# A spectral filter fused with a gated feed-forward: the forward sine table exchanged by DMA instead of TensorE

## The chip, the cores and the metric

The kernel runs on one core of a Trainium2 chip. TensorE (PE) does matrix products, VectorE (DVE) and ScalarE (ACT) do element-wise work and move results out of PSUM, GpSimd (POOL) does small integer and constant work, SyncE (SP) issues every DMA. The metric is the device time of one execution in microseconds (us). "Faster" or "slower" always means against the kernel before.

## The reference

```python
def _A_ref(x, w_r, w_i):
    X = rfft2(x.astype(float32), axes=(-2, -1))
    X = X * (w_r + 1j * w_i)
    return irfft2(X, s=(S, D), axes=(-2, -1)).astype(bfloat16)

def _B_ref(x, w_gate, w_up, w_down):
    return (_gelu(x @ w_gate) * (x @ w_up)) @ w_down

x = A_x                          # 1 x 2048 x 640, bfloat16
xn = _layernorm(x, axis=-1)
s = _A_ref(xn, A_w_r, A_w_i)
g = _silu(_B_ref(xn, B_w_gate, B_w_up, B_w_down))    # F = 1536
return x + s * g
```

A row-wise layer norm feeds two branches. One is a two-dimensional Fourier transform over 2048 rows and 640 columns, a product with a complex filter, and the transform back. The other is a feed-forward network with a GELU gate. Their product is added to the input.

## The kernel before

The 2048 rows are held as 16 slabs X[:, n1, :] of 128 rows. A 2048-point transform along the rows is split into 128 points times 16 points.

**Feed-forward.** Four groups of four slabs. For each group, `ffn_piece` (L707) makes 12 tiles of gate and up products (L714), ACT applies GELU (L718), VectorE multiplies (L720). `down_third` (L729) multiplies with the down weights (L738). xnT, the transposed normalized input of a group, comes from `slab_T` (L458): the first four slabs by TensorE, the other twelve by a DMA transpose that SyncE issues (L465).

**Forward spectral part.** VectorE folds pairs of slabs (L443 to L453). `slab_S1` (L480) does the 128-point step along the rows: five matmuls per slab into pz (L484) whose moving operand is the slab's block Tfwd[:, n1, :] of a sine table. `group_D` (L504) does the step along the columns (pd, L494 and L498) and stores Z to a DRAM scratch ZDR (L512).

**16-point phase.** `load_B2` (L524) reads ZDR back in another layout (L530); it starts when the last Z store has landed. Then eleven bursts: `s2_in` (px, L556) transforms, ACT evicts (L564), VectorE multiplies with the filter W1 and W2 (L568), `s2_out` (pu, L583) transforms back, and the result goes to a second scratch. Burst 0 begins at place `sb` of the plan below. `load_V` and the whole inverse part are placed relative to `sb`.

**Inverse part.** `slab_S1i` (L626) uses the blocks Tinv[:, n1, :] of the inverse table (pv, L631). `group_Di`, `group_cs` and `group_Y` follow, and `finish` (L682) multiplies and adds (L689, L690) and stores to the output (L691).

**The tables.** Integer phases in vt are made by GpSimd and VectorE. `tinv_sin` (L319) turns all 16 blocks into Tinv, 128 x 2048, in one ACT instruction (L320). `tfwd(h)` (L322) makes the forward table: it transposes eight 128 x 128 blocks of Tinv on TensorE (L326) into a PSUM tile, and VectorE copies them into Tfwd (L327). It is called for h = 0 and 1.

**Filter loads.** `w_rows(i, hh, ri, pm)` (L112) loads an eighth of filter W1 (i = 0) or W2 (i = 1): two DMAs, or three where one is cut in two (L118, L120, L121, L123), about 160 KB each. k = 0 to 7 stands for the eight calls that load W1, k = 8 to 15 for W2. GpSimd halves the edge columns of W1 and W2 (L127, `w_edge`).

**The order of the work** is written out by hand. `back` is a list of 144 pieces of feed-forward work (places 0 to 143). After place s of that list the program issues what `put(s, ...)` filed there, in the order of the `put` calls. A place is one third of a down product (8 matmuls) or one gate or up tile (5 matmuls). Places 24 to 35 are the down products of group 0, 36 to 59 the gate and up tiles of group 1, and 60 to 71 its down products. Every engine's instructions, and SyncE's DMA issues, keep the order of the places.

The places that matter here, before the change: `w_rows` of k = 0 to 7 at places 8 to 15, one each; `slab_T` of slabs 4 to 7 at 17, 19, 21 and 23; `tinv_sin` at 23; `tfwd` at 26 and 27; `slab_S1` of slab 0 at 30, of 1 to 3 at 32 to 34, of 4 to 6 at 37 to 39, of 7 to 9 at 42 to 44, of 10 to 12 at 47 to 49; `slab_T` of slab 8 at 32; `load_B2` at 56; `sb` = 65.

Of the kernel before, what the change touches and what calls it, by code (L numbers as in the profile page):

```python
# [10 lines left out]
BF16 = mybir.dt.bfloat16  # L11
INT32 = mybir.dt.int32
ACT = mybir.ActivationFunctionType
ALU = mybir.AluOpType
P = 128
# [11 lines left out]
TWO_PI = 2.0 * math.pi  # L27
# [4 lines left out]
def kernel(  # L32
# [40 lines left out]
    with tc.manual_schedule():  # L73
        build(nc, locals())


def build(nc, env):
    consts, big, wts, xg, work, psA, psB = (env[k] for k in ("consts", "big", "wts", "xg", "work", "psA", "psB"))
# [51 lines left out]
    Tinv = consts.tile([P, NS, P], BF16)  # L130
    Tfwd = consts.tile([P, NS, P], BF16)
# [5 lines left out]
    ident = consts.tile([P, P], BF16)  # L137
# [4 lines left out]
    def gtile(shape, dt):  # L142
        n = 1
        for k in shape:
            n *= k
        w = n if dt != BF16 else n // 2
        ap = GEN[:, goff[0]:goff[0] + w]
        goff[0] += w
        assert goff[0] <= NH * L // 2
        if dt != INT32:  # L150
            ap = ap.bitcast(dt)
        if len(shape) > 1:
            names = "abcdefg"[:len(shape)]
            ap = ap.rearrange("p (%s) -> p %s" % (" ".join(names), " ".join(names)), **dict(zip(names, shape)))
        return ap

    def c1(name, dt=FP32):
        return consts.tile([P, 1], dt, name=name)
# [44 lines left out]
    negpi = c1("negpi")  # L203
# [13 lines left out]
    vt = gtile([NS, P], INT32)  # L217
# [98 lines left out]
    def silu_table():  # L316
        nc.scalar.activation(out=warm, in_=negpi, func=ACT.Silu)

    def tinv_sin():  # L319
        nc.scalar.activation(out=Tinv, in_=vt, func=ACT.Sin, bias=negpi, scale=TWO_PI / 2048.0)  # L320

    def tfwd(h):  # L322
        sl = slice(8 * h, 8 * h + 8)
        pt = psB.tile([P, 8, P], BF16, tag="b")
        for k in range(8):
            nc.tensor.transpose(out=pt[:, k, :], in_=Tinv[:, 8 * h + k, :], identity=ident)  # L326
        nc.vector.tensor_copy(out=Tfwd[:, sl, :], in_=pt)  # L327

    fv = gtile([10, LH], FP32)
    ftm = gtile([5, LH], FP32)  # L330
# [464 lines left out]
    def put(s, *item):  # L795
        plan[s].append(item)
# [24 lines left out]
    put(17, stats, 8)  # L821
    put(19, stats, 9)
    put(23, fold_a, 0)
    for it in ((silu_table,), (tinv_sin,), (ft_sin, 0)):
        put(23, *it)
    put(24, fold_b, 0)
    put(28, mg_mask)
    put(25, root, 8, 2)
    put(25, fold_a, 1)
    put(26, tfwd, 0)  # L830
    put(27, tfwd, 1)
    put(27, norm, 8)
    put(28, fold_b, 1)
    put(29, stats, 10)
# [24 lines left out]
    for pair in range(6):  # L859
        b = F0 + 3 * pair + (0 if pair < 4 else 3)  # L860
        put(b, fold_a, pair + 2)
        put(b + 1, fold_b, pair + 2)
    z_end = F0 + 26
# [1 line left out]
        put(32 + 3 * k, slab_T, 8 + k, 2)  # L865
        put(65 + 3 * k, slab_T, 12 + k, 2)
    for k in range(16):
        put(8 + k if k < 8 else (32, 35, 38, 41, 44, 44, 47, 47)[k - 8], w_rows, k // 8, k % 8 // 4, k % 2, k % 4 // 2)
    put(40, w_edge, 0)
    put(z_end + 4, w_edge, 1)  # L870
    put(z_end, load_B2)
    put(z_end + 3, mg_turn)
    sb = z_end + 9
    for b in range(len(BURSTS)):
        put(sb + 24 * b // 11, s2_in, b)
        if b > 0:
# [69 lines left out]
```

## Time and profile before

| | before |
|---|---|
| median of 3 runs | 204.14 us (204.1 to 204.27) |
| the profiled execution's own time | 204.42 us |
| its span (first to last instruction) | 202.6 us |
| PE / DVE / ACT / POOL busy | 195.6 / 129.3 / 122.4 / 33.4 us |
| granted TensorE clock | 1.000 |
| DMA | 31.77 MB, mean 157 GB/s, hardware queue 71.4% of 16 engines |

The span is what the profile sees; the execution's own time has some 1.8 us around it. "Busy" is the sum of an engine's working time. Matrix products are pipelined, so a row's mean duration (219 ns for 128 columns) is longer than the pitch at which such products follow one another. The chain of work that ended last is traced back from the last instruction, at each step to what released it. A wait in SyncE's own list is one in front of a DMA issue. "To landing" is the time from the start of a DMA's issue until its data has arrived. A releaser can be named wrongly where a wait has several semaphores.

### The profile page before, as it was taken

What the parts mean: (1) busy time and instruction counts of PE and PEld (TensorE: products, weight loads), DVE (VectorE), ACT (ScalarE), POOL (GpSimd) and SP (SyncE); (2) the same over time, 40 slices, a digit from 0 to 9 for tenths busy, and PEclk for the clock granted to TensorE, in tenths of its full rate; (3) what the DMA queues carried; (4) which work ended last, traced back from release to release, by engine and by line L of the source; (5) the groups of instructions that cost most, each with busy time, mean ns of one, the idle gap of its engine ahead of it and who ended that gap; (6) DMA issues with size and microseconds to landing.
All of it is one profiled execution on the core that took longest, in us unless ns stands there. A gap on an engine that the chain in (4) does not pass through costs nothing.

```text
span 202.6 us, 4209 instructions
## 1 busy us (share of the span) xinstructions
PE 195.6 (97%) x1574; PEld 119.8 (59%) x1589; DVE 129.3 (64%) x340; ACT 122.4 (60%) x208; POOL 33.4 (16%) x61
## 2 busy tenths in 40 slices
PE   7899999999999999999999999999999999999993
PEld 5688854777555555566644333457775555556762
DVE  7886966786488982533576465342358776867672
ACT  2448657857886768423788688425375647476631
POOL 5327779953000200100000000000000000000000
PEclk9999999999999999999999999999999999999999
DMA  5999999899799999729995233569501334224211
GB/s 167 306 297 305 372 310 142 158 147 137 153 170 143 173 174 174 180 43 226 213 228 111 44 97 101 130 164 317 172 0 68 97 102 127 69 92 144 86 69 60
DMA packets 43315, 31.77 MB, mean 157 GB/s; under 512 B 12192, under 2 KB 41504, under 8 KB 43296
## 3 DMA queue, kind: packets, MB, share of 16 engines
q1 hardware_dynamic: 43296, 31.52, 71.4%
q8 instruction: 12, 0.20, 0.4%
q14 instruction: 7, 0.06, 0.1%
HBM read 21.66 MB, written 7.88 MB: 146 GB/s over the span
## 4 chain that ended last, share of the span: by engine, by line
PE 90%; DVE 4%; DMA 2%; issue 1%; POOL 1%; SPq 0%; ACT 0%; DVEq 0%
PE psu L714 25%; PE psg L714 24%; PE psg L738 13%; PE psu L738 12%; PE pd L494 5%; PE pz L484 2%; PE pv L631 2%; PE pu L583 2%; DMA X<-in_A_x_dram 2%; PE px L556 2%; PE pd L498 2%; DVE st L174 1%; DVE uT L720 1%; POOL rst L190 1%; PE pt L326 0%
## 5 line engine op out<-in xcount | busy, mean ns | idle before, releaser
L714 PE MATMUL psu<-xnT,Wu 128*128 128x512 bf16 (+2 forms) x289 | 60.9, 339 | 0.6 <-issue 0.2
L714 PE MATMUL psg<-xnT,Wg 128*128 128x512 bf16 (+2 forms) x286 | 60.4, 338 | 0.9 <-issue 0.5
L720 DVE TENSOR_TENSOR uT<-psu,ge 128x512 bf16<-128x512 f32 (+2 forms) x59 | 34.3, 585 | 29.8 <-PE psu L714 22.5
L718 ACT ACTIVATE ge<-psg 128x512 bf16<-128x512 f32 (+2 forms) x59 | 30.5, 518 | 27.6 <-PE psg L714 25.9
L738 PEld LDWEIGHTS <-uT 128*128 128x128 bf16 x384 | 36.3, 98 | 14.6 <-issue 0.6
L714 PEld LDWEIGHTS <-Wu 128*128 128x128 bf16 x295 | 26.6, 98 | 22.9 <-issue 2.7
L714 PEld LDWEIGHTS <-Wg 128*128 128x128 bf16 x295 | 26.6, 98 | 21.9 <-issue 1.5
L738 PE MATMUL psg<-Wd,uT 128*128 128x320 bf16 (+1 forms) x192 | 30.3, 302 | 0.0
L738 PE MATMUL psu<-Wd,uT 128*128 128x320 bf16 (+1 forms) x192 | 29.2, 296 | 0.0
L568 DVE TENSOR_TENSOR X<-xs,W 128x972 bf16<-128x972 bf16 (+2 forms) x22 | 13.3, 646 | 10.6 <-ACT xs L564 10.6
L174 DVE BATCH_NORM_STATS2 st<-X 128x6 f32<-128x320 bf16 x32 | 14.2, 482 | 0.5 <-DMA X<-in_A_x_dram 0.3
L633 ACT CAST W<-pv 128x640 bf16<-128x640 f32 x16 | 11.1, 692 | 5.4 <-PE pv L631 5.4
L510 ACT CAST GEN<-pd 128x966 bf16<-128x966 f32 (+1 forms) x10 | 10.4, 1102 | 5.3 <-PE pd L498 5.3
L656 ACT ACTIVATE W<-pd 128x960 bf16<-128x960 f32 (+2 forms) x14 | 10.1, 780 | 5.0 <-PE pd L498 5.0
L486 ACT CAST GEN<-pz 128x640 bf16<-128x640 f32 x16 | 11.0, 697 | 3.2 <-PE pz L484 3.2
L589 ACT CAST X<-pu 128x486 bf16<-128x486 f32 (+4 forms) x22 | 12.3, 558 | 0.3
L564 ACT CAST xs<-px 128x972 bf16<-128x972 f32 (+2 forms) x11 | 10.3, 936 | 2.4 <-PE px L556 2.4
L190 POOL TENSOR_TENSOR rst<-ve,mhalf 128x1 f32<-128x1 f32 (+2 forms) x9 | 6.5, 717 | 29.5 <-DVE ve L188 29.5
L662 DVE TENSOR_TENSOR W<-W 128x960 bf16<-128x960 bf16 (+1 forms) x12 | 6.8, 599 | 4.8 <-ACT W L656 4.8
L689 DVE TENSOR_TENSOR Yall<-Yall,G 128x640 bf16<-128x640 bf16 (+3 forms) x18 | 8.1, 450 | 2.1 <-ACT G L743 1.9
L747 DVE SCALAR_TENSOR_TENSOR G<-th,psu 128x320 bf16<-128x320 f32 x8 | 3.9, 488 | 8.4 <-ACT th L746 8.4
L452 DVE TENSOR_TENSOR f<-uvt 128x512 bf16<-128x512 bf16 x16 | 6.7, 421 | 3.0 <-PE pz L484 2.9
(137 smaller groups left out, 202.5 us busy)
## 6 DMA issues: line engine op xcount, KB each, us to landing
ZDR<-GEN SPq DMA_DIRECT2D x16, 160.5 KB, 5.3
xt<-in_A_x_dram SPq DMA_DIRECT2D x8, 320.0 KB, 3.5
UDR<-X SPq DMA_DIRECT2D x10, 240.8 KB, 3.6
W<-in_A_w_r_dram SPq DMA_DIRECT2D x14, 160.5 KB, 7.7
W<-in_A_w_i_dram SPq DMA_DIRECT2D x14, 160.5 KB, 6.0
out_dram<-Yall SPq DMA_DIRECT2D x14, 160.0 KB, 1.8
B<-ZDR SPq DMA_DIRECT2D x8, 240.8 KB, 5.5
Vin<-UDR SPq DMA_DIRECT2D x6, 321.0 KB, 6.3
```

The lines of the kernel that those rows point to most:

```text
L174: nc.vector.bn_stats(out=st[:, k, :], in_=X[:, n1, 320 * k:320 * k + 320])
L486: nc.scalar.copy(out=Zt[n1], in_=pz)
L494: nc.tensor.matmul(out[a][g], lhsT=lhs[a][:, g, :], rhs=T[:, g, 0:w], start=(a == 0), stop=False)
L510: ev(out=zd.rearrange("p a c (m b) -> p a c m b", b=2)[:, :, :, :, b], in_=pd[b])
L564: nc.scalar.copy(out=xs, in_=px[:, :, 0:n * w].rearrange("p k (h l) -> p k h l", l=w))
L568: nc.vector.tensor_tensor(out=pp[-1], in0=xs, in1=WT[:, :, h0:h0 + n, l0:l0 + w], op=ALU.mult)
L589: nc.scalar.copy(out=us[:, :, :, c0:c0 + (w + 1 - m) // 2], in_=pv[:, :, :, m:w:2])
L633: nc.scalar.copy(out=vs, in_=pv)
L714: nc.tensor.matmul(ps, lhsT=WT[:, c, t * P:(t + 1) * P], rhs=xnT[g][:, c, c0:c1_], start=(c == 0), stop=(c == 4))
L718: nc.scalar.activation(out=ges[t], in_=ps, func=ACT.Gelu_apprx_tanh)
L720: nc.vector.tensor_tensor(out=uT[g][:, t, c0:c1_], in0=ps, in1=ges[t], op=ALU.mult)
L738: nc.tensor.matmul(ph, lhsT=uT[g][:, t, j * P:(j + 1) * P], rhs=Wd[:, t, c0:c1_], start=(t == 0), stop=(t == NT - 1))
```

## The change

The forward table's blocks are turned by four DMA transposes (SyncE's queue) of four blocks each, straight from Tinv into Tfwd, with no PSUM tile and no copy. The sine is computed in two halves of eight blocks. The transfers stand at places 23 to 26, behind the sine. The filter loads k = 4 to 7 move from places 12 to 15 to places 27 to 30. The 16-point phase, and with it the loads and pieces of the inverse part, stands one place later (`sb` = 66).

```diff
-    def tinv_sin():
-        nc.scalar.activation(out=Tinv, in_=vt, func=ACT.Sin, bias=negpi, scale=TWO_PI / 2048.0)
-
-    def tfwd(h):
+    def tinv_sin(h):
         sl = slice(8 * h, 8 * h + 8)
-        pt = psB.tile([P, 8, P], BF16, tag="b")
-        for k in range(8):
-            nc.tensor.transpose(out=pt[:, k, :], in_=Tinv[:, 8 * h + k, :], identity=ident)
-        nc.vector.tensor_copy(out=Tfwd[:, sl, :], in_=pt)
+        nc.scalar.activation(out=Tinv[:, sl, :], in_=vt[:, sl, :], func=ACT.Sin, bias=negpi, scale=TWO_PI / 2048.0)
+
+    def tfwd(q):
+        sl = slice(4 * q, 4 * q + 4)
+        nc.sync.dma_start_transpose(out=Tfwd[:, sl, :], in_=Tinv[:, sl, :].rearrange("p n k -> p (n k)"))
...
-    for it in ((silu_table,), (tinv_sin,), (ft_sin, 0)):
+    for it in ((silu_table,), (tinv_sin, 0), (tinv_sin, 1), (ft_sin, 0)):
         put(23, *it)
...
-    put(26, tfwd, 0)
-    put(27, tfwd, 1)
+    for q in range(4):
+        put(23 + q, tfwd, q)
...
     for k in range(16):
-        put(8 + k if k < 8 else (32, 35, 38, 41, 44, 44, 47, 47)[k - 8], w_rows, k // 8, k % 8 // 4, k % 2, k % 4 // 2)
+        put((8 + k if k < 4 else 23 + k) if k < 8 else (32, 35, 38, 41, 44, 44, 47, 47)[k - 8], w_rows, k // 8, k % 8 // 4, k % 2, k % 4 // 2)
...
-    sb = z_end + 9
+    sb = z_end + 10
```

## The prediction

> **What bounds the kernel now.** I read the page first: shares by engine, then the chain of work that ended last.
>
> ```profile
> PE 195.6 (97%) x1574; PEld 119.8 (59%) x1589; DVE 129.3 (64%) x340; ACT 122.4 (60%) x208; POOL 33.4 (16%) x61
> ...
> PE 90%; DVE 4%; DMA 2%; issue 1%; POOL 1%; SPq 0%; ACT 0%; DVEq 0%
> ```
>
> TensorE is busy for 97% of the span and is 90% of the chain. A TensorE instruction removed after about 14 us shortens the span by its pitch; a wait put in front of one lengthens it by its length, for nothing later has slack to give back. So two questions decide: what the removed transposes took on TensorE, and whether the first matmul that reads Tfwd has to wait. Second view: the chain in order of time (start, length), around the exchange.
>
> ```profile
> 38.48 0.45 PE pt L326 x8
> 38.93 1.09 PE psg L738 x8
> 40.02 0.45 PE pt L326 x8
> ...
> 42.63 1.09 PE psg L738 x8
> 43.72 0.28 PE pz L484 x5
> ```
>
> Both groups of eight transposes stand on the chain, 0.45 us each, and the first reader of Tfwd (pz, L484, place 30) follows closely. TensorE's timeline has that matmul's start at 43.56, as does the list of Tfwd's users. Third view: SyncE's queue, since the new transfers are issued there.
>
> ```profile
> 34.38 0.57 SPq L123 DMA_DIRECT2D W<-in_A_w_r_dram  x1
> 35.52 3.41 SPq L118 DMA_DIRECT2D W<-in_A_w_r_dram  x4
> 38.98 2.74 SPq L123 DMA_DIRECT2D W<-in_A_w_r_dram  x4
> 41.89 7.95 SPq L465 DMA_TRANSPOSE xnT<-X  x4
> 49.94 0.53 SPq L512 DMA_DIRECT2D ZDR<-GEN  x1
> 50.56 1.21 SPq L465 DMA_TRANSPOSE xnT<-X  x1
> ```
>
> SyncE runs late. The eight issues from 35.52 to 41.7 are filter loads k = 4 to 7, asked for at places 12 to 15; the four transposed slabs behind them (slab_T of 4 to 7, places 17 to 23) go out at 41.89 to 49.83, though their data was normalized by 33.4 (ACT's timeline, L434). An issue starts when the eighth before it has landed: the load at 28.77 starts as Wd lands (18.34 + 10.4), the one at 35.52 as the load of 23.17 lands (+ 12.3).
>
> **The change, part by part.**
>
> *Transposes off TensorE.* 16 matmuls, 2 x 0.45 = **-0.90 us** on the chain. With everything before it unchanged, pz would be reached at 43.56 - 0.90 = 42.66.
>
> *Copies off VectorE, sine in two.*
>
> ```profile
> L320 ACT ACTIVATE Tinv<-GEN,negpi 128x2048 bf16<-128x2048 int32 x1 | 2.0, 1987 | 0.0
> ...
> L327 DVE COPY Tfwd<-pt 128x1024 bf16<-128x1024 bf16 x2 | 1.4, 692 | 1.0 <-PE pt L326 1.0
> ```
>
> VectorE loses 2 x 0.69 us; it waits on TensorE here, so 0. The sine of 128 columns (L397) takes 0.392, of 2048 1.987: 0.83 ns a column and 0.29 fixed. Each part is then 1.14, ACT carries +0.29, and the first part ends at 36.20 + 1.14 = 37.34. ACT's next evictions (L743, 38.85 and 39.17) go 0.3 later; their banks are written again at 42.5 or later, so 0. Without that cover it would cost 0.3.
>
> *SyncE's order.* With k = 4 to 7 at places 27 to 30, SyncE reaches slab_T(4) at 35.52. Then come slab_T 5, 6, 7, the four Tfwd transfers (places 23 to 26), the eight issues of k = 4 to 7, the Z store of place 31 and slab_T(8). Only the first transfer is urgent: it holds slabs 0 to 3. The others are read at places 37, 43 and 49, 8 us and more later.
>
> When does it land? Its source (37.34) is not the limit; four slab transfers ahead of it are. *Early end:* each issues in 1.22 us when nothing holds it (1.23 at 48.60, 1.21 at 50.56), 1.27 with the step between: 35.52 + 4 x 1.27 = 40.6. The new transfer has four blocks instead of five, an estimated 0.97 from 1.22. The slab issued at 48.60 landed 2.76 later, 1.53 after its issue ended. So 40.6 + 0.97 + 1.53 = 43.1. *Late end:* the four slabs did not issue freely; they took 7.95 us and stood behind seven unfinished filter loads. Then the last filter load landed at 41.11 + 7.8 = 48.9 and the fourth slab's issue ended at 49.83, 0.92 after it. Now too seven loads are unfinished at 35.52, the last landing at 34.38 + 6.3 = 40.7. That gives 41.6, and 41.65 + 0.97 + 1.53 = 44.15. If the transfer took the median of line 465 (5.2) or its longest (8.8) it would land at 46.9 or 50.5; those stood in a fuller queue. I take 44.0, near the second value, because the queue ahead is the same in kind and number. The stall at pz is 44.0 - 42.66 = **+1.3 us**; bounds 0.4 and 1.5, far ends 4.2 and 7.8. Behind pz in TensorE's order is everything else, so all of it counts.
>
> Here a rule of the Trainium skill speaks against the change. "VectorE: DVE Perf Modes", section "The three transpose paths", gives 1309 ns for one 128x128 block by DMA against 390 ns on TensorE, and advises TensorE. By it four blocks are an estimated 5.2 us, the landing would be 46.9 and the sum +3.1 instead of +0.2. The trace disagrees on both: 0.45 us for eight blocks on TensorE, and the last two slabs of five blocks land 0.65 us apart (45.88 + 4.84 and 48.60 + 2.76).
>
> *Filter loads later.* The four loads occupied the queue for some 8.2 us (landings 40.7 to 48.9) and now do so from about 47 to 55.4. W1 is first read after 94, so its own lateness costs 0. POOL's edge scaling (L127, 50.28) waits to about 56 with the root for slabs 12 and 13 behind it, due at place 41, about 58: covered. But stores and loads behind them go 2 to 3 us later. What absorbs this (busy per engine, then clock, DMA share, GB/s):
>
> ```profile
> 51.40:58.00 6.60, 6.55 (x55) 3.49 (x54) 3.11 (x11) 5.90 (x8) 0.00 (x0) 1.00 0.88 177
> 58.00:82.00 24.00, 23.71 (x204) 13.85 (x204) 17.84 (x46) 16.60 (x23) 1.59 (x2) 1.00 1.14 166
> 82.00:85.00 3.00, 2.84 (x26) 1.43 (x26) 1.49 (x3) 1.78 (x2) 0.52 (x1) 1.00 0.48 107
> ```
>
> The queue is full from 58 to 82 and half empty from 82 to 85, before the last Z stores (83.8, waiting for VectorE): some 1.5 us of room there and 0.8 before 58. I take 0; bounds 0 and +1.
>
> *16-point phase a place on.* A place here is eight down matmuls, 1.09 us. Its first matmul waits for B now: five matmuls of burst 0 span 0.83 where those of burst 1 span 0.40.
>
> ```profile
> 93.52 0.83 PE L556 MATMUL px<-B,MG 64*64 64x162 bf16 x5
> ...
> 96.55 0.40 PE L556 MATMUL px<-B,MG 64*64 64x159 bf16 x5
> ```
>
> The spacing beyond an ordinary tile change is 0.2 us; the place removes it: **-0.2**, and leaves B about 0.9 us for being late. All later pieces move by one place as well, TensorE's amount unchanged. At the end VectorE's last group (193.43 to 197.11) goes 1.09 later, to 198.2, still ahead of the last product at 198.79: 0, and 0.1 if it slips that far.
>
> *Sum:* -0.90 + 1.3 + 0 - 0.2 = **+0.2 us**. The profiled execution took 204.42 (span 202.6, 1.8 around it), so 204.6 for it; it ran 0.28 over the median of the runs, 204.14, which becomes **204.35**.
>
> **Rivals.**
>
> *In time (faster).* The slabs issue freely once k = 4 to 7 are gone, and the transfer lands by 43.3. For it: 1.21 to 1.23 us per issue in two rows. Against: the slabs issued at 43.42 and 45.88 took 2.36 and 2.63, with a like queue ahead. Stall 0.4 to 0.65, sum about -0.6: 203.5.
>
> *Late transfer (slower).* The first transfer lands like the median of its kind, 5.2 us after issue, at 46.9; TensorE stands at pz for 4.2 us. Sum 4.2 - 0.9 - 0.2 = +3.1: 207.2. It decides from a landing later than 44.15: beyond that the stall eats the gain and 0.4 more. For it: median 5.2. Against: by then the queue ahead is only slabs. The page above says the same time.
>
> *Backlog reaches B (slower).* The 2 to 3 us by which the queue lags at 56 do not find room; the last Z stores, then B, land 2 us late. TensorE comes to px at 93.52 + 1.09 + 0.4 (the changed sum ahead) = 95.0, B's second part at 93.95 + 2: stall 1.0, sum +1.2: 205.35. Against: the half-empty stretch at 82 to 85.
>
> *Doesn't do it:* the transfers would wait behind filter loads after all. SyncE issues in the order of the places, so I give it nothing.
>
> **How the numbers follow.** About 0.2% (0.41 us) is what a measurement of this kernel can tell from no change. Forecast 0.42, of which 0.36 within 0.2% and 0.06 slower; in time 0.28; late transfer 0.15; backlog 0.15. Faster 0.28, same 0.36, slower 0.36. The forecast's own range is 203.75 to 204.75, from stalls of 0.7 to 1.7. To hold 8 in 10 the range takes in the first rival and the third and part of the second: 203.4 to 206.5.
>
> **What would show it.** No line 326 or 327; slab_T(4) issued at 35.5; the first new transfer issued at 40.6 to 41.7 and landed at 43.1 to 44.2; a gap before the first pz of 0.4 to 1.5 us, none before the later ones; px of burst 0 as short as burst 1's; the last Z stores within 1 us of where they were. The forecast is wrong if the gap at pz is under 0.7 or over 1.7, or if px of burst 0 waits.

## The result, and the profile after

The changed kernel takes 212.62 us (median of six executions, 209.87 to 214.51) against 204.12 for the kernel before beside it: ratio 1.0364, 95% interval 1.0328 to 1.0399. Ratios, here and in the table below, leave out executions over 1.5% slower than the fastest of the same kernel, two of the six here, which is why 3.64% (7.4 us) is less than the 8.5 us between the medians. The forecast was no clear change, 204.35 us; the changed kernel is slower and lies outside the stated range. In all six executions the mean granted clock is below full, 0.976 to 0.992. The profiled execution took 213.03 us, its span is 211.1. Line numbers behind `tfwd` are two lower in the changed kernel: pz is L482, px L554, the slab transposes L463, the new transfers L325.

The page of the changed kernel (busy time by engine, the granted clock in 40 slices, the chain by engine):

```profile
PE 198.9 (94%) x1573; PEld 119.7 (57%) x1573; DVE 127.7 (60%) x338; ACT 122.2 (58%) x209; POOL 33.7 (16%) x61
...
PEclk9999999999999999999599999999999999999999
...
PE 67%; DMA 18%; DVE 7%; SPq 3%; issue 1%; ACT 1%; POOL 1%; DVEq 0%
```

TensorE was 90% of the chain and is now 67%. DMA has 18%, and in one slice the clock is at a half. The chain in order of time and SyncE's list show the exchange itself:

```profile
42.32 1.09 PE psg L736 x8
43.40 0.28 PE pz L482 x5
```

```profile
35.04 5.36 SPq L463 DMA_TRANSPOSE xnT<-X  x4
40.50 5.16 SPq L325 DMA_TRANSPOSE Tfwd<-Tinv  x4
45.70 3.57 SPq L118 DMA_DIRECT2D W<-in_A_w_r_dram  x4
49.32 2.56 SPq L123 DMA_DIRECT2D W<-in_A_w_r_dram  x4
51.99 0.54 SPq L510 DMA_DIRECT2D ZDR<-GEN  x1
```

The transposes are gone from the chain and pz follows the down product without a pause. The first transfer, issued at 40.50, landed 2.5 us later, at 43.0, just ahead of its reader at 43.24. Where the time went stands 50 us later, at the first matmuls of the 16-point phase (TensorE's timeline; in brackets the idle time before and its releaser):

```profile
94.41 1.25 PE L736 MATMUL psg<-Wd,uT 128*128 128x320 bf16 x8
99.40 0.55 PE L554 MATMUL px<-B,MG 64*64 64x162 bf16 x3 [3.74 <-DMA B<-ZDR]
100.58 0.61 PE L554 MATMUL px<-B,MG 64*64 64x486 bf16 x2 [0.64 <-DMA B<-ZDR]
```

TensorE waits 4.4 us for B. The columns of the next view are PE, PEld, DVE, ACT and POOL busy, then the granted clock, the DMA share (the times of packets overlap, so it can exceed 1) and GB/s:

```profile
97.00:99.00 2.00, 0.00 (x0) 0.00 (x0) 0.00 (x0) 0.00 (x0) 0.00 (x0) 1.00 0.93 228
99.00:106.40 7.40, 6.37 (x35) 3.22 (x36) 1.95 (x4) 2.07 (x4) 0.00 (x0) 0.54 1.09 209
106.40:109.00 2.60, 2.60 (x29) 1.61 (x25) 1.46 (x4) 2.20 (x4) 0.00 (x0) 1.00 1.06 219
```

After the wait the clock is at 0.54 for 7.4 us (at 0.50 for 6.8 of them). That takes 7.4 x 0.46 = 3.4 us at most; TensorE stood idle for 0.64 us of it, so some 3.1 us of work is lost. The Trainium skill, "TensorE: Matmul & The Clock Gate", Part 1, states that an idle window of some 3.4 us halves the clock until a busy one has passed. The trace agrees: 3.74 us of idle did it, and the waits of 0.6 to 1.3 us in the profiles below did not.

The account against the profile of before: 4.4 of wait for B less the 0.4 there was, 3.1 of clock, 0.56 at another stall, -0.90 for the transposes, +0.57 at the start of the execution (the second group of transposes of the input begins at 9.02 instead of 8.45, in code that is unchanged; in the runs below it begins at 8.07 to 8.34, so this belongs to the one execution). That is 7.3 of the 8.5 us between the spans; some 1.2 is spread over smaller waits.

Why is B late? The same view of the changed kernel, and then of the kernel before:

```profile
41.00:48.00 7.00, 7.00 (x66) 5.15 (x65) 4.92 (x17) 4.61 (x10) 3.96 (x11) 1.00 0.54 84
48.00:58.00 10.00, 10.00 (x88) 6.06 (x85) 6.25 (x21) 8.38 (x12) 0.86 (x1) 1.00 1.16 161
58.00:82.00 24.00, 23.41 (x201) 13.47 (x200) 17.11 (x46) 16.10 (x23) 2.12 (x3) 1.00 1.23 161
82.00:92.00 10.00, 9.74 (x74) 5.68 (x73) 4.03 (x8) 3.06 (x5) 0.52 (x1) 1.00 1.21 173
```

```profile
41.00:48.00 7.00, 7.00 (x64) 5.08 (x62) 4.77 (x17) 4.89 (x10) 3.00 (x10) 1.00 1.37 122
...
82.00:92.00 10.00, 9.84 (x75) 6.08 (x75) 4.03 (x8) 3.26 (x6) 0.52 (x1) 1.00 0.47 111
```

From 41 to 48 us the DMA engines are half idle (share 0.54) where they were full (1.37). SyncE spends that time issuing transposes, 1.3 us each with the step between, and up to 45.70 nothing else is issued. The DMA lines of the changed kernel from 41 to 48 us, in 40 slices of 0.175 us, show it:

```profile
DMA  9300799600029992000799600079999400000000
GB/s 215 55 0 1 161 222 212 145 8 0 0 51 224 212 211 52 0 0 1 157 221 219 142 9 0 0 154 197 205 196 43 0 0 3 7 10 9 10 9 0
```

Each of the four transfers moves data for some 0.7 of its 1.3 us. The moved loads are issued from 45.70 on, but from 46.4 to 48 almost nothing moves (0 to 10 GB/s), and the first of them lands at 50.4. By slab_T(8) the queue is 5.9 us late (landing 59.2 against 53.4), and it stays full to 92. The lateness bites twice: ACT's last eviction before the Z stores waits for an earlier Z store to leave its buffer (VectorE's, beside it, starts at 86.16 as well), and so the last Z stores are issued late and then stand in a full queue.

```profile
86.14 1.24 ACT L508 CAST GEN<-pd 128x966 bf16<-128x966 f32 x1 [4.64 <-DMA ZDR<-GEN]
```

An earlier wait of this kind is the 0.56 us stall:

```profile
77.40 0.44 PE L482 MATMUL pz<-Tfwd,f 128*128 128x128 bf16 x5 [0.56 <-ACT GEN L508]
```

SyncE's list at the end of the forward part, first in the changed kernel, then in the kernel before:

```profile
83.16 5.71 SPq L510 DMA_DIRECT2D ZDR<-GEN  x6
95.64 1.94 SPq L528 DMA_DIRECT2D B<-ZDR  x3
```

```profile
83.81 1.41 SPq L512 DMA_DIRECT2D ZDR<-GEN  x3
89.00 3.24 SPq L530 DMA_DIRECT2D B<-ZDR  x5
```

The last Z store landed at 88.38 + 7.0 = 95.4 instead of 88.9, and B after it.

### The profile page after: what moved, and what is told of

It is laid out like the page before. It is cut to its first block, busy times and chain, and to the rows that moved or that the text cites. A ratio compares the mean times of both kernels' runs of the same rounds, so it can differ in the third digit from the quotient of the medians.

```text
span 211.1 us, 4200 instructions
## 1 busy us (share of the span) xinstructions
PE 198.9 (94%) x1573; PEld 119.7 (57%) x1573; DVE 127.7 (60%) x338; ACT 122.2 (58%) x209; POOL 33.7 (16%) x61
## 4 chain that ended last, share of the span: by engine, by line
PE 67%; DMA 18%; DVE 7%; SPq 3%; issue 1%; ACT 1%; POOL 1%; DVEq 0%
PE psg L712 18%; PE psu L712 18%; PE psu L736 10%; PE psg L736 10%; DMA ZDR<-GEN 7%; DMA W<-in_A_w_i_dram 7%; PE pd L492 3%; DMA X<-in_A_x_dram 2%; PE pu L581 2%; PE pv L629 2%; DMA B<-ZDR 2%; PE px L554 2%; SPq L510 2%; DVE st L174 2%; PE pd L496 1%
## 5 line engine op out<-in xcount | busy, mean ns | idle before, releaser
L712 PE MATMUL psg<-xnT,Wg 128*128 128x512 bf16 (+2 forms) x295 | 61.5, 340 | 0.1
L736 PEld LDWEIGHTS <-uT 128*128 128x128 bf16 x384 | 37.2, 100 | 16.5 <-issue 1.0
L736 PE MATMUL psg<-Wd,uT 128*128 128x320 bf16 (+1 forms) x192 | 31.1, 306 | 0.1
L736 PE MATMUL psu<-Wd,uT 128*128 128x320 bf16 (+1 forms) x192 | 30.5, 307 | 0.0
L554 PE MATMUL px<-B,MG 64*64 64x486 bf16 (+6 forms) x46 | 5.3, 408 | 4.4 <-DMA B<-ZDR 4.4
```

What stands on the lines that cost most here:

```text
L712: nc.tensor.matmul(ps, lhsT=WT[:, c, t * P:(t + 1) * P], rhs=xnT[g][:, c, c0:c1_], start=(c == 0), stop=(c == 4))
L736: nc.tensor.matmul(ph, lhsT=uT[g][:, t, j * P:(j + 1) * P], rhs=Wd[:, t, c0:c1_], start=(t == 0), stop=(t == NT - 1))
```

## The experiments

The theory to be tested, **starved queue**: the eight transposes, one issue of 1.25 us each, keep SyncE from feeding the DMA engines, and the delay of the loads behind runs through the full queue to B; the wait for B is paid a second time by the clock. Rivals: moving the loads is enough by itself; the later place costs time; and transposes by DMA burden the queue wherever they stand. The diffs are against the changed kernel unless another is named.

| run | median, us | before beside it | ratio (95%) |
|---|---|---|---|
| loads back early | 213.79 | 203.88 | 1.0492 (1.0472 to 1.0513) |
| table by TensorE | 204.12 | 203.88 | 1.0012 (1.0002 to 1.0021) |
| phase a place back | 211.70 | 203.88 | 1.0348 (1.028 to 1.0415) |
| two transfers | 207.12 | 203.88 | 1.0192 (1.0113 to 1.0271) |
| wait filled with matmuls | 207.84 | 203.71 | 1.0204 (1.0183 to 1.0225) |
| interleaved order | 203.48 | 203.71 | 0.9987 (0.9976 to 0.9998) |
| loads by GpSimd | 206.88 | 203.71 | 1.0174 (1.0138 to 1.0211) |
| interleaved, place back | 204.38 | 203.89 | 1.0016 (0.9994 to 1.0037) |
| interleaved, four transfers | 204.08 | 203.89 | 1.0012 (0.9987 to 1.0037) |
| slabs 8 to 11 off the queue | 206.43 | 203.89 | 1.0121 (1.0092 to 1.015) |
| slabs 8 to 11 in a row | 205.05 | 203.68 | 1.0065 (1.0045 to 1.0085) |
| interleaved, slabs in a row | 203.15 | 203.68 | 0.9967 (0.9955 to 0.9979) |

### Loads back early

```diff
-        put((8 + k if k < 4 else 23 + k) if k < 8 else ...
+        put(8 + k if k < 8 else ...
```

> The changed kernel with the four filter loads back at places 12 to 15. Theory 'starved queue' (the loads, issued behind eight transposes of 1.25 us each, leave the DMA engines half idle from 41 to 48 us, and the delay runs on through the queue to B): no wait at px for B, but the first transfer is issued only at about 50 and lands at about 52.4, so TensorE waits some 9 to 10 us at the first pz and its clock drops after it: about 214 to 217 us. Rival 'transfers burden the queue' (blocks turned by DMA slow the queue wherever they stand): a wait at px as well, over 217.

```profile
51.45 0.69 PE L482 MATMUL pz<-Tfwd,f 128*128 128x128 bf16 x5 [8.98 <-DMA Tfwd<-Tinv]
```

213.79 us, just under the expected range. The transfers wait behind the loads, TensorE waits 9 us for the first of them (the clock is at 0.50 from 46 to 55), and nothing waits for B. Without the move the exchange costs as much elsewhere, and the burden rival's second wait does not appear.

### Table by TensorE

The sixteen transposes and two copies of the kernel before, with the other parts of the change left in:

```diff
-    def tfwd(q):
-        sl = slice(4 * q, 4 * q + 4)
-        nc.sync.dma_start_transpose(...
+    def tfwd(h):
+        sl = slice(8 * h, 8 * h + 8)
+        pt = psB.tile([P, 8, P], BF16, tag="b")
+        for k in range(8):
+            nc.tensor.transpose(out=pt[:, k, :], in_=Tinv[:, 8 * h + k, :], identity=ident)
+        nc.vector.tensor_copy(out=Tfwd[:, sl, :], in_=pt)
...
-    for q in range(4):
-        put(23 + q, tfwd, q)
+    put(26, tfwd, 0)
+    put(27, tfwd, 1)
```

> The changed kernel with the forward table made by TensorE and VectorE as before (places 26 and 27); the moved loads, the sine in two and the later 16-point phase stay. Starved queue: SyncE is past the slab transposes at 40.4 and issues the loads 5 us earlier than in the changed kernel; B is late by 1.5 us at most, px waits under 1 us, the clock stays full: 204 to 205.3 us. Rival 'moving the loads is enough by itself': B as late as in the changed kernel, 210 to 213 us.

204.12 us. SyncE issues the loads right behind the slabs, px does not wait (its five matmuls span 0.40):

```profile
40.49 2.54 SPq L118 DMA_DIRECT2D W<-in_A_w_r_dram  x4
43.08 3.72 SPq L123 DMA_DIRECT2D W<-in_A_w_r_dram  x4
```

```profile
94.46 0.40 PE L557 MATMUL px<-B,MG 64*64 64x162 bf16 x5
```

So the moved loads, the sine in two and the later place together cost 0.12%; the four transfers in front of the loads make the rest. "Moving the loads is enough" falls.

### Phase a place back

```diff
-    sb = z_end + 10
+    sb = z_end + 9
```

> The changed kernel with the 16-point phase back by one place. Starved queue: B lands when it did, px waits about 1.1 us longer, so the total is the same as the changed kernel's within its spread, 210 to 214 us. Rival 'the later place costs time': faster than the changed kernel by 1 us or more in span, with the same wait.

211.70 us, the same as the changed kernel within its spread. The wait at px is 4.28 + 0.56 us there; it grew by 0.5 and not by 1.1, since in that execution TensorE came to px 2.5 us earlier and B landed 2 us earlier. The place neither costs nor helps while the wait for B is longer than it.

### Two transfers

```diff
-        sl = slice(4 * q, 4 * q + 4)
+        sl = (slice(0, 4), slice(4, NS))[q]
...
-    for q in range(4):
+    for q in range(2):
```

> The changed kernel with two transfers, of 4 and of 12 blocks, in place of four of 4. Starved queue with an issue cost per transfer (1.22 to 1.26 us for 4 blocks and 1.22 to 1.33 for 5): the second transfer issues in about 1.3 us, the loads start 2.5 us earlier, B lands 2.5 us earlier, px waits about 1.9 us and the clock stays full: 205 to 206.5 us. If the issue goes by blocks, the second takes 3.7 us and nothing changes: 210 to 213. Rival 'transfers burden the queue': 210 to 213 as well.

```profile
40.48 2.61 SPq L325 DMA_TRANSPOSE Tfwd<-Tinv  x2
43.14 2.99 SPq L118 DMA_DIRECT2D W<-in_A_w_r_dram  x4
```

Twelve blocks issue in 1.30 us where four take 1.22: the cost on SyncE is per transfer. The loads start 2.6 us earlier. The profiled execution, the fastest of the four, waits 0.72 us at px and its clock stays at 1.00. The median, 207.12, lies 0.6 over the expectation, with a spread of 205.1 to 209.2: in two executions the mean clock is 0.990 and 0.992, so there B was still late enough to drop it. The direction is as expected, the gain less.

### The wait filled with matmuls

```diff
+        if b == 0:
+            pw = psB.tile([P, 2, 512], FP32, tag="b", name="pw")
+            for _ in range(32):
+                nc.tensor.matmul(pw[:, 0, 0:256], lhsT=ident, rhs=Tinv[:, 0:2, :], start=True, stop=True)
         px = psB.tile([P, 2, 512], FP32, tag="b")
```

> The changed kernel with 32 more matmuls of 256 columns (3.4 us at full clock, into a PSUM tile that nothing reads) ahead of the first matmul of the 16-point phase, where TensorE waits for B. Theory 'the wait is paid twice' (the changed kernel's profile has TensorE's clock at 0.50 for 6.8 us after the 3.7 us wait, which is 3.4 us of work lost): the wait stays, filled, the clock stays at 1.00, the time falls by some 3.4 us to about 208.5 to 209.5. Rival 'the clock costs nothing, the queue sets the time': 212.

```profile
94.15 3.66 PE L551 MATMUL pw<-Tinv,ident 128*128 128x256 bf16 x32
97.74 0.40 PE L558 MATMUL px<-B,MG 64*64 64x162 bf16 x5
```

```profile
94.00:98.00 4.00, 4.00 (x40) 3.27 (x37) 0.22 (x1) 0.00 (x0) 0.00 (x0) 1.00 1.08 223
98.00:106.00 8.00, 8.00 (x77) 5.07 (x74) 5.01 (x9) 6.23 (x11) 0.00 (x0) 1.00 1.11 208
```

207.84 us, 0.7 under the expectation. With 3.7 us of work that computes nothing in place of the wait, the clock stays at 1.00 and the ratio falls from 1.0364 to 1.0204, 1.6% or 3.3 us. That the clock costs something is shown by this; how much is not, since in the profiled execution B is asked for at 91.71 instead of 95.64 and is there before the filling ends. The 3.1 us rest on the changed kernel's own profile.

### Interleaved order

Two transfers, of blocks 0 to 3 and of blocks 4 to 15, and loads and slabs in turn:

```diff
-        sl = slice(4 * q, 4 * q + 4)
+        sl = (slice(0, 4), slice(4, NS))[q]
...
-        put(17 + 2 * k, slab_T, 4 + k, 2)
+        put((17, 19, 24, 25)[k], slab_T, 4 + k, 2)
...
-    for q in range(4):
-        put(23 + q, tfwd, q)
+    put(23, tfwd, 0)
+    put(26, tfwd, 1)
...
-        put((8 + k if k < 4 else 23 + k) if k < 8 else ...
+        put((8 + k if k < 4 else 19 + k) if k < 8 else ...
```

> Two transfers (4 and 12 blocks) and SyncE's order changed: slab transposes 4 and 5, the first transfer, loads k=4, slab 6, loads k=5, slab 7, loads k=6, the second transfer, loads k=7. Starved queue: the DMA engines have loads to move while transposes issue, B lands within 1.5 us of where it did before the change, the first transfer lands ahead of pz, so the 0.9 us of transposes are gained: 203 to 204 us. Rival 'transfers burden the queue' (a DMA transpose between loads stalls the engines until all have drained): B is late by 3 us or more, 206 to 210.

```profile
38.02 1.22 SPq L325 DMA_TRANSPOSE Tfwd<-Tinv  x1
39.29 1.23 SPq L118 DMA_DIRECT2D W<-in_A_w_r_dram  x2
40.56 1.29 SPq L463 DMA_TRANSPOSE xnT<-X  x1
41.90 1.24 SPq L118 DMA_DIRECT2D W<-in_A_w_r_dram  x2
```

```profile
93.40 0.80 PE L554 MATMUL px<-B,MG 64*64 64x162 bf16 x5
```

```profile
41.00:48.00 7.00, 7.00 (x67) 5.15 (x65) 5.74 (x20) 4.44 (x11) 3.16 (x10) 1.00 1.25 152
```

203.48 us, 0.13% under the kernel before. The same transfers and loads as in the run with two transfers, only in another order: the DMA share from 41 to 48 is 1.25, pz does not wait, and px waits 0.4 as it did before the change. The burden rival expected 206 or more.

### Loads by GpSimd

```diff
+        eng = nc.gpsimd if i == 0 and hh == 1 else nc.sync
...
-                nc.sync.dma_start(out=WT[...
+                eng.dma_start(out=WT[...
```

> The changed kernel, four transfers of 4 blocks, with the moved loads k=4 to 7 issued by GpSimd at the same places instead of SyncE. Starved queue by SyncE's issue time: the loads go out beside the transposes, the DMA engines are busy from 41 to 48, B lands within 1.5 us of where it did before the change: 203 to 204.7 us. Rival 'transfers burden the queue': loads and transposes hold each other up, the first transfer is late too: 208 or more.

206.88 us: a miss. The engines are fed (share 0.93 from 41 to 48), yet the later transfers land 5.1, 7.9 and 7.1 us after their issue, and px waits 0.75 us in the profiled execution, the fastest of the four; in two others the mean clock is 0.992. So there is something in the burden rival: loads and transposes in flight together hold each other up, and SyncE's issue time is not the whole of the loss.

### Interleaved, place back

Against the interleaved order:

```diff
-    sb = z_end + 10
+    sb = z_end + 9
```

> The interleaved order with the 16-point phase back by one place. In the interleaved run the first px matmul starts at 93.40 and waits 0.4 us for B, as before the change. Theory 'B decides, the place covers it': px comes 1.1 us earlier, B does not, so TensorE waits 1.1 us more and what the exchange gained is lost: 204.3 to 204.8 us. Rival 'the place itself costs, the queue has room': 203.2 to 203.6.

204.38 us, within what the first theory expected: with the queue in order, B decides and the place is what covers it. This is weak: the interval reaches below 1, and in the profiled execution, the fastest, the five matmuls of px span 0.65 us, so the longer wait is not seen there.

### Interleaved, four transfers

Against the interleaved order, with four blocks in each transfer:

```diff
-        sl = (slice(0, 4), slice(4, NS))[q]
+        sl = slice(4 * q, 4 * q + 4)
...
-    put(23, tfwd, 0)
-    put(26, tfwd, 1)
+    for q, at in enumerate((23, 26, 27, 28)):
+        put(at, tfwd, q)
```

> The interleaved order, but with four transfers of four blocks (the second ahead of loads k=7, the third and fourth behind them) instead of 4 and 12. Starved queue: two more issues of 1.25 us, with loads waiting in the queue behind which they hide; B up to 1 us later: 203.5 to 205 us. Rival 'each transfer burdens the queue by itself': B 2 us or more later than with two transfers, over 205.5.

204.08 us, within the expectation, but the spread (203.1 to 205.4) and a wait of 0.89 + 0.75 us at px in the slowest execution leave the two theories unseparated here.

### Slabs 8 to 11 off the queue

The last argument chooses TensorE and VectorE in place of the DMA:

```diff
-        put(32 + 3 * k, slab_T, 8 + k, 2)
+        put(32 + 3 * k, slab_T, 8 + k, 0)
```

> The changed kernel with the transposed slabs 8 to 11 made by TensorE and VectorE instead of DMA (20 transposes, 1.1 us of TensorE). It tells what a DMA transpose costs in a loaded queue. If a slab costs only its own 0.6 us of the engines, B lands 2.5 us earlier than in the changed kernel, px waits about 1.5 us, no clock loss: 206 to 207.5. If transposes hold the queue up (1.2 us and more each), B lands 5 us or more earlier and px does not wait: 204.3 to 205.3.

206.43 us, which is the time that the first expectation named, but not for its reason: px does not wait (B is asked for 4.3 us earlier, and TensorE comes 1.1 later). TensorE waits elsewhere, 0.53 at pz and 1.32 at the first of these transposes, and 20 transposes cost 1.1. The queue tells more: the third group's last Z store lands at 68.2 instead of 76.0. Three slabs less ahead of it (8, 9 and 10) gained 7.8 us, of which 1.3 were gained ahead of them (the last moved load landed at 56.9 instead of 58.1): some 2 us a slab, for 0.6 us of data. The DMA lines of the changed kernel from 62.5 to 65.9 us, in 40 slices of 0.085 us, show such a hold:

```profile
DMA  9999999999999009000100000010499999010000
GB/s 95 94 163 367 120 133 154 157 226 111 54 45 18 9 9 15 0 0 0 9 6 9 9 9 9 9 12 9 108 286 313 310 346 175 6 8 8 8 8 8
```

For 1.4 us almost nothing moves (0 to 18 GB/s), then half a microsecond at about 300: the slab. The same view lists two transfers that are not the kernel's own data:

```profile
q14 instruction: 1, 0.01, 3.7%
q8 instruction: 1, 0.02, 2.5%
```

That these hold the slab up, and not the loads ahead of it, is a rival that no run tests. None has to be in flight for a hold: in the profile of before, from 47.5 to 48.6 us, ahead of the transposed slabs, only 17 GB/s move in the mean, and the view of these 1.1 us lists none. What they add to the 1.4 us is open.

### Slabs 8 to 11 in a row

```diff
-        put(32 + 3 * k, slab_T, 8 + k, 2)
+        put(36, slab_T, 8 + k, 2)
```

> The changed kernel with the DMA transposes of slabs 8 to 11 issued one behind the other at place 36 instead of at places 32, 35, 38 and 41 between loads. In the run with these slabs off the queue, the Z stores of the third group landed 7.9 us earlier than in the changed kernel, 2 us a slab, though a slab's own data take 0.6. Theory 'a transpose behind loads holds the queue until every engine has drained': in a row they are held once, B lands 3 to 5 us earlier than in the changed kernel and px waits under 1.5 us: 203.5 to 206 us. Rival 'a transpose costs 2 us wherever it stands': 210 to 213.

```profile
57.65 6.20 SPq L463 DMA_TRANSPOSE xnT<-X  x4
...
89.03 6.48 SPq L528 DMA_DIRECT2D B<-ZDR  x10
```

```profile
93.87 0.40 PE L554 MATMUL px<-B,MG 64*64 64x162 bf16 x5
```

205.05 us, 3% faster than the changed kernel by moving four issues. The four slabs land 0.5 to 0.8 us apart, and B is asked for at 89.03 instead of 95.64, 6.6 us earlier where 3 to 5 were expected. So in this run the hold comes once, at the change from loads to transposes, and not with each transpose. The profiled execution is the fastest; the spread is 203.6 to 207.7.

### Interleaved, slabs in a row

Against the interleaved order:

```diff
-        put(32 + 3 * k, slab_T, 8 + k, 2)
+        put(36, slab_T, 8 + k, 2)
```

> The interleaved order (two transfers, loads between) with the slabs 8 to 11 in a row at place 36. Theory as in the run with the slabs in a row: the last 0.4 us wait for B goes as well: 202.9 to 203.5 us. Rival: no difference from the interleaved order, 203.2 to 204.

```profile
PE 196.0 (97%) x1573; PEld 119.2 (59%) x1573; DVE 127.8 (64%) x338; ACT 122.5 (61%) x209; POOL 33.7 (17%) x61
```

```profile
93.42 0.40 PE L554 MATMUL px<-B,MG 64*64 64x162 bf16 x5
```

203.15 us, ratio 0.9967 (0.9955 to 0.9979): faster than the kernel before, by 0.3%, and than the changed one. The rival's range began at 203.2, so the time alone does not decide between the two; the span of px does, 0.40 instead of 0.80. TensorE has no wait at pz or px left. The gain between the medians is 0.5 us of the 0.9 that the transposes took; where the rest went is not shown.

## Why the prediction was wrong

*Transposes off TensorE, -0.90.* Right. In the interleaved run pz starts at 42.36, 1.2 earlier than before, 0.3 of it from the start of that execution.

*The stall at pz, +1.3.* Mis-sized: 0 in the changed kernel's profile and 0.3 to 0.75 in the runs that kept its order of slabs and first transfer. The 0 is luck, since that execution was 0.57 late from its start: the transfer landed at 43.0, and 42.66, where pz was to be reached, would have left 0.3. I took the late end, because the queue ahead was the same in number; but the slabs issued in 1.22 to 1.33 us each, as the early end had it. The early end held by two errors that cancel: the transfer's issue took 1.22 (four blocks save nothing), not 0.97, and it landed 1.25 after its issue, not 1.53.

*Filter loads later, taken at 0 with bounds 0 and +1.* This is the step that failed. The prediction let the loads land from about 47 to 55.4, called the queue 2 to 3 us late at 56, and took that as absorbed before B. The last moved load landed at 58.1, the queue was 5.9 late at slab_T(8) and 6.5 at the last Z store, and TensorE waited 4.4 us for B. The 8.2 us for the eight loads came from the profile of before, where they stood in a full queue. I did not see that a queue into which SyncE issues only transposes runs half empty (share 0.54), because the issue, 1.3 us, is longer than the data, some 0.7, nor that the loads do not follow a transpose at once (0 to 10 GB/s from 46.4 to 48). The fourth transfer landed only at 48.3, 2.7 us after its issue ended, where its sisters took 1.25. A transfer named "instruction", of 0.02 MB, stands beside it in the DMA view; in the run with the slabs off the queue none does while the fourth transfer is in flight, and there it takes no longer than its sisters. That this is the reason was not tested. How much of the lateness is issue time and how much is holding each other up is open as well: with the loads issued by GpSimd half of the loss stayed (1.0174).

The room that the prediction found, 0.8 before 58 and 1.5 after 82, is there for a smaller lateness: the interleaved run is 2.5 late at slab_T(8) (landing 55.9) and asks for B at 89.08, as before. In the changed kernel none of the 5.9 was absorbed.

*The rival "backlog reaches B"* named the mechanism, the place and the releaser. It had a chance of 0.15, and its price was 1.0 of wait; the wait was 4.4, and I did not reckon with what a wait of that length does to the clock, some 3.1 more. The interleaved run shows both gone when the queue is in order, the filled run a full clock when the wait is filled.

*Place on, -0.2 and 0.9 of room.* The wait to be removed was 0.4, not 0.2: from the first px to the next down product it is 0.75 us before the change and 0.33 in the run with the table by TensorE. That the place covers about a microsecond of B's lateness is likely and not shown: the interleaved run with the place back is slower by 0.9 us in the median, but the two intervals meet. In the changed kernel there was far more to cover.

*The late-transfer rival,* and with it the sum by the Trainium skill's 1309 ns a block ("VectorE: DVE Perf Modes", "The three transpose paths"): no run shows it. In the run with two transfers, twelve blocks landed 3.7 us after the start of their issue, 0.3 us a block with the issue in it. The advice of the Trainium skill (same page, "Rules for kernel authors"), TensorE where the result may go to PSUM, held for the changed kernel all the same (1.0012 against 1.0364), for a reason that the page does not give; it did not hold for the interleaved order with the slabs in a row (0.9967).

## What to carry to other kernels

When work moves from a busy engine to a DMA, count the issuing queue's time as well as the data: a transfer whose issue takes longer than its data (here 1.3 us against some 0.7) starves the queue, and what stands behind it is late, to the next place where an engine waits for a load. Put such issues between plain loads while the queue has a reserve, make them few and large, and keep transposes together. Where a wait on TensorE as long as the 3.7 us here is in sight, price the clock with it.

## What the runs showed of the hardware

A DMA transpose costs SyncE 1.22 to 1.26 us for 4 blocks of 128 x 128, 1.21 to 1.33 for 5 and 1.30 for 12 when nothing holds it. Around one transpose between loads almost nothing moved for 1.1 us (before) and 1.4 us (changed kernel), the second time with transfers named "instruction" beside it, though four transposes in a row landed 0.5 to 0.8 us apart. That a transpose waits until every engine has drained the loads ahead is my reading; no run here shows an engine by itself. A wait of 3.74 us halved TensorE's clock for 6.8 us after it; waits up to 1.3 us left it at 1.00.
